# Whole-array transposes and halved products of h in a fused RWKV-7 and SoLU kernel

## The chip, the cores and the metric

The kernel runs on one NeuronCore of a Trainium2 chip. The metric is the device time of one execution in microseconds (us). The core's engines each run a list of instructions of their own: TensorE (PE in the profile; PEld is its loading of weights), VectorE (DVE), ScalarE (ACT), GpSimd (POOL), and SyncE (SP), which here only issues DMAs. TensorE writes its results into PSUM, which ACT and DVE read; a PSUM bank holds 512 fp32 columns.

## The reference

A recurrent attention block feeds an MLP. Everything is fp32 (the two weight matrices arrive as 64-bit floats and are converted on the chip).

```python
B, H, S, D = 4, 8, 768, 40
for t in range(S):                         # state: (B, H, D, D)
    y[:, :, t] = einsum('bhd,bhde->bhe', rt, state)
    Sa = einsum('bhde,bhe->bhd', state, at)
    state = state * wt[:, :, None, :] - einsum('bhd,bhe->bhde', Sa, bt) \
            + einsum('bhd,bhe->bhde', vt, kt)
x = y.transpose(0, 2, 1, 3).reshape(B * S, H * D)      # 3072 x 320
h = x @ w_in                                           # 320 -> 1024
e = exp(h - max(h));  solu = h * e / (sum(e) + 1e-9)
ln = (solu - mean) / sqrt(var + 1e-6) * g_ln
out = ln @ w_out                                       # 1024 -> 320
```

## The kernel before

The 768 time steps are cut into 12 chunks of C = 64, and the four batches into two pairs. One work item is one chunk of one pair: 2 batches x 64 tokens = 128 partitions, batch 0 on partitions 0 to 63 and batch 1 on 64 to 127 (`half(p)`). There are N = 24 items. The recurrence inside a chunk is turned into products of 64x64 matrices and the inverse of a triangular matrix; the inverse is worked out column by column on DVE (`invert`, the groups prod and uu of lines 516 and 519).

All instructions are in a hand-written order, per engine (`manual_schedule`). After a start-up (lines 884 to 970) one loop (line 973) runs i from -1 to 26. Iteration i works on several items at once: it prepares item j = i+5 (decay, transposes of a and b), starts item i+1 (transposes of k, v, r and the state, scores), finishes the attention of item i, and does the MLP of items c = i-2 (h, maximum, exp, variance) and c-1 (transposes and output product). Iterations from i = 5 on (`EARLY - AHEAD`) take the second branch of the loop, which the text calls steady; a steady iteration is the stretch from one transposition of e (tile plnT) to the next.

On TensorE most products are of 64x64 matrices in a quarter of the array, four of them side by side: two halves of the rows (the batch or the head that is contracted) and two halves of the columns. An fp32 product is executed as two passes, so each appears twice in the profile; a transpose appears once.

What the change touches:

- `turned` (line 395) transposes one tensor of 128 tokens x 8 heads x 64 columns. Two heads stand side by side, of which W2 = 104 columns are taken, so there are four blocks; each block is transposed for batch p = 0 and p = 1 by its own instruction. Each loads 64 rows x 104 columns of data as weights and streams the 64 columns of the identity. The two instructions of a block sit on different halves of the array's rows and write to different PSUM banks (`t` is [128, 2, 512]: p chooses the bank, y the 256 columns within). A tensor thus fills half of both banks, and the result is seen as [104, p, j, t].
- It is called by `decay_turned` (tensor ei), `front` (a), `front_b` (b, from the tile kb), `attend_kv` (k from kb, and v), `attend_r` (r) and `stated` (the state, st). Each gives back the copy out of PSUM, which is issued later (on ACT, or on DVE for a and b).
- `folded` (line 794) transposes e, 128 tokens x 1024, in eight blocks of 128 columns for each p into tile plnT; its copy to lnT (line 809) puts the batches side by side. `folded_last` (line 812) does so for the last item, in two tiles.
- `decay_by_halves` (line 368) multiplies the logarithms of the decay with a triangular matrix in 64x64 tiles, the two column halves of 160 in the two banks of the tile that the state's transposes share.
- `hidden` (line 740) does one fifth, n, of h = x @ w_in: four products (row half x, token half y) of 512 columns each. `SPLITS` says how many of the four are done in two of 256 columns instead, for every n and item; its entry 24 holds for all items without an entry of their own.

In a steady iteration TensorE does, in order: transposes of a, b (tile pa), k, v (pkv); the last two of eight output products of an earlier item (po, four records each); transposes of e (plnT), the state (pst), r, ei (pb); the decay products (pst); pu; ps; three fifths of h; and so on to pyo and the first six output products (po).

Of the kernel before, what the change touches and what calls it, by code (L numbers as in the profile page):

```python
# [17 lines left out]
P = 128  # L18
C = 64
# [5 lines left out]
EARLY = 10  # L25
NK = 5
FIRST = 6
SPLITS = {2: (0, 0, 0, 2, 4), 24: (0, 0, 0, 0, 2)}


LN_EXP = "natural_log_exp_and_others"
# [22 lines left out]
def kernel(  # L54
# [18 lines left out]
    nc = tc.nc  # L73
# [6 lines left out]
    NF = DFF // P  # L80
    W2 = C + D
# [17 lines left out]
    def c_(name):  # L99
        lo, hi = where[name]  # L100
        return cst[:, lo:hi]

    ident, tri = c_("ident"), c_("tri")
# [20 lines left out]
    for x in ex_t:  # L124
# [10 lines left out]
                          in_=c_("eye_hi").unsqueeze(1).to_broadcast([P, 8, Q]))  # L135
# [9 lines left out]
    def pair(tag, name):  # L145
        return psum.tile([P, 2, 512], FP32, tag=tag, name=name)
# [121 lines left out]
    def half(p):  # L268
        return slice(C * p, C * p + C)
# [14 lines left out]
    def mm(o, lhsT, rhs, start=True, stop=True):  # L284
        nc.tensor.matmul(o, lhsT=lhsT, rhs=rhs, start=start, stop=stop, skip_group_check=True)  # L285
# [28 lines left out]
    def ok(i):  # L314
        return 0 <= i < N
# [52 lines left out]
    def decay_by_halves(i, t):  # L368

        if not ok(i):  # L370
            return lambda: None
        d = st[i]
        width = DM // 2
        t = t[:, :, 256:256 + width]
        for x in range(2):
            for p in range(2):
                mm(t[half(p), x], c_("cum")[half(p), half(p)], d["lw"][half(p), width * x:width * x + width])

        def evict():
            nc.scalar.activation(out=ei_t[0].rearrange("p (x h) d -> p x h d", x=2)[:, :, :, 0:D],  # L380
                                 in_=t.rearrange("p x (h d) -> p x h d", d=D), func=AF.Exp)
            inv = d["inv"] = two.tile([P, DM], FP32, tag="inv", name="inv", bufs=4)
            nc.scalar.activation(out=inv.rearrange("p (x n) -> p x n", x=2), in_=t, func=AF.Exp, scale=-1.0)
        return evict
# [9 lines left out]

    def turned(t, y, x, skip=0):

        at = 256 * y
        for j in range(4):
            for p in range(2):
                nc.tensor.transpose(out=t[0:W2, p, at + C * j:at + C * j + C],  # L400
                                    in_=x[half(p), 2 * j:2 * j + 2].rearrange("p a b -> p (a b)")[:, skip:skip + W2],
                                    identity=ident[half(p), half(p)])
        return t[0:W2, :, at:at + 256].rearrange("p b (j t) -> p b j t", j=4)

    def tokens(name, bufs=1):
        return two.tile([P, 2, 4, C], FP32, tag=name, name=name, bufs=bufs)
# [6 lines left out]
    def decay_turned(i, t=None, y=0):  # L413

        if not ok(i):
            return lambda: None
        ex = st[i]["ex"] = ex_t[i % (AHEAD + 2)]
        t = turned(pair("B", "pei") if t is None else t, y, ei_t[0])
        return lambda: nc.scalar.copy(out=ex[0:W2, :, :, 1:], in_=t)

    def front(i, t=None, y=0):
        if not ok(i):
            return lambda: None
        d = st[i]
        t = turned(pair("C", "pa") if t is None else t, y, d["raw_a"])
        aT = d["aT"] = tokens("aT", AHEAD)
        return lambda: nc.vector.tensor_tensor(out=aT[0:W2], in0=t, in1=d["ex"][0:W2, :, :, 0:C], op=ALU.mult)

    def front_b(i, t=None, y=0):
        if not ok(i):  # L430
            return lambda: None
        d = st[i]
        t = turned(pair("A", "pb") if t is None else t, y, d["kb"][:, H:])

        def evict():
            if i < EARLY:
                d["bT"] = kept("bT", t)
            else:
                d["bT"] = tokens("bT")
                nc.vector.tensor_copy(out=d["bT"][0:W2], in_=t)  # L440
        return evict
# [132 lines left out]
    def attend_kv(i, t):  # L574

        if not ok(i):
            return lambda: None
        d = st[i]
        for y, x in enumerate((d["kb"], v_t[0])):
            turned(t, y, x)  # L580
        o = two.tile([P, 2, 8, C], FP32, tag="kvT", name="kvT", bufs=1)
        d["kT"], d["vT"] = o[:, :, 0:4], o[:, :, 4:8]
        return lambda: nc.scalar.copy(out=o[0:W2].rearrange("p b j t -> p b (j t)"), in_=t[0:W2])

    def attend_r(i, t, y):
        if not ok(i):
# [153 lines left out]
    def hidden(i, n):  # L740
# [7 lines left out]
        quads = [(y, x) for y in range(2) for x in (y, 1 - y)]  # L748
        whole = len(quads) - SPLITS.get(i, SPLITS[N])[n]
        for part, some in ((slice(0, 512), quads[:whole]), (slice(0, 256), quads[whole:]), (slice(256, 512), quads[whole:])):  # L750
# [43 lines left out]
    def folded(i):  # L794
        if not ok(i):
            return lambda: None
        d = st[i]
        if i == N - 1:
            return folded_last(d)
        lnT = d["lnT"] = two.tile([P, NF, P], FP32, tag="lnT", name="lnT", bufs=1)  # L800
        t = pair("h" if i < N - LAG - 2 else "A" if i == N - LAG - 2 else turn["Y"], "plnT")
        for f in range(NF):
            for p in range(2):
                nc.tensor.transpose(out=t[:, p, f * C:f * C + C], in_=d["e"][half(p), f * P:(f + 1) * P],  # L804
                                    identity=ident[half(p), half(p)])

        def evict():
            o, y = lnT.rearrange("q f (p t) -> q p f t", p=2), t.rearrange("q p (f t) -> q p f t", f=NF)
            nc.scalar.copy(out=o, in_=y)
        return evict  # L810

    def folded_last(d):
        n = NF // 2
        d["lnT"] = (two.tile([P, 2 * n, P], FP32, tag="kvT", name="lnT", bufs=1),
                    two.tile([P, 2 * n, P], FP32, tag="lnT", name="lnT", bufs=1))
        ts = pair(turn["Y"], "plnT"), pair("A", "plnT")
        for f in range(NF):
            for p in range(2):
                nc.tensor.transpose(out=ts[f // n][:, p, f % n * C:f % n * C + C],
                                    in_=d["e"][half(p), f * P:(f + 1) * P], identity=ident[half(p), half(p)])  # L820

        def evict():
            for copy, lnT, t in zip((nc.vector.tensor_copy, nc.scalar.copy), d["lnT"], ts):
                copy(out=lnT[:, 0:n].rearrange("q f (p t) -> q p f t", p=2),
                     in_=t[:, :, 0:n * C].rearrange("q p (f t) -> q p f t", f=n))
        return evict

    def output_last(i):
# [144 lines left out]
    for i in range(-1, N + LAG + 1):  # L973
        j, c = i + AHEAD, i - LAG
# [17 lines left out]
        if i < EARLY - AHEAD:  # L992
            tc_, ta = pair("C", "pa"), pair("A", "pb")
            front_out, r_out = front(j, ta, 0), attend_r(i + 1, ta, 1)
            fold_out = folded(c - 1)
            ei_out, b_out = decay_turned(j + 1, tc_, 0), front_b(j, tc_, 1)
            kv_out = attend_kv(i + 1, pair(turn["X"], "pkv"))
            r_out()
            front_out()
# [11 lines left out]
        else:  # L1011
            turn.update(zip("XY", ("BC", "CB")[(i - EARLY + AHEAD) % 2]))
            ta = pair("A", "pa")
            front_out, b_out = front(j, ta, 0), front_b(j, ta, 1)
            kv_out = attend_kv(i + 1, pair(turn["Y"], "pkv"))
            front_out()
            kv_out()
            b_out()
            if i == N + LAG:
                fold_out = folded(c - 1)  # L1020
# [8 lines left out]
            if i < N + LAG:  # L1029
                fold_out = folded(c - 1)  # L1030
            ts = pair("A", "pst")
# [3 lines left out]
            if i == EARLY - AHEAD and ok(j + 2):  # L1035
                logged(j + 2)
            cum_out = decay_by_halves(j + 2, ts)
            for evict in (r_out, ei_out, fold_out, s_out, *late):
                evict()
# [129 lines left out]
```

## Time and profile before

| | us |
|---|---|
| median of three runs | 538.33 (538.08 to 539.39) |
| span of the profiled execution | 536.5 |
| PE busy | 480.7 |
| DVE busy | 430.6 |
| ACT busy | 314.1 |
| PE, products of h (1064 records) | 121.7 |
| PE, output products po (768 records) | 115.2 |
| PE, transposes of e (368 records, all but the last item) | 16.3 |

The profile is of one execution. Busy time is the union of an engine's instructions, idle time is what lies between them. PE instructions are pipelined: each lasts longer in the records than it keeps the array from the next one, so rates are read from start to start. The times that the three runs show include some time around the span.

### The profile page before, as it was taken

The numbers are of one execution on the slowest core, as the hardware profiler recorded it, in microseconds if no ns is written. First come the engines' busy times: TensorE is split into PE (matmuls) and PEld (weight loads), VectorE is DVE, ScalarE is ACT, GpSimd is POOL, SyncE is SP. The second block draws the span as 40 slices with busy tenths as digits, with TensorE's granted clock in tenths as the row PEclk, the third lists the DMA queues.
The fourth block names the chain that finished last, engine by engine and source line by source line (L and its number), as shares of the span: only waits on it lengthen the run. The fifth ranks groups of instructions, "written<-read, shape, count | busy, mean of one in ns | idle before, by whom it ended". The sixth has DMA issues, their size and how long they took to land.

```text
span 536.5 us, 28053 instructions
## 1 busy us (share of the span) xinstructions
PE 480.7 (90%) x12029; PEld 391.0 (73%) x12029; DVE 430.6 (80%) x1752; ACT 314.1 (59%) x627; POOL 227.0 (42%) x376
## 2 busy tenths in 40 slices
PE   4633775798989999999999999999999999999997
PEld 3522665665878878877887887788778877887766
DVE  4599987999997987997998979979989888544322
ACT  3633466488457566556666665666656555654433
POOL 4577538245253344545445263544445331210300
PEclk9999978799999999999999999999999999999999
DMA  8898889765465566674774776675554551421210
GB/s 149 153 157 160 177 142 206 165 134 124 90 131 120 102 125 138 123 151 96 147 156 104 132 150 121 118 155 109 114 118 102 108 111 43 106 65 29 61 53 24
DMA packets 194475, 63.95 MB, mean 119 GB/s; under 512 B 166840, under 2 KB 186528, under 8 KB 194352
## 3 DMA queue, kind: packets, MB, share of 16 engines
q1 hardware_dynamic: 181232, 41.60, 41.8%
q0 software_dynamic: 10768, 19.95, 15.2%
q8 instruction: 94, 1.54, 1.2%
q10 hardware_dynamic: 2352, 0.62, 0.7%
q14 instruction: 29, 0.24, 0.2%
HBM read 47.96 MB, written 14.16 MB: 116 GB/s over the span
## 4 chain that ended last, share of the span: by engine, by line
PE 73%; DVE 17%; DMA 5%; issue 2%; ACT 2%; SPq 0%; POOL 0%; ACTq 0%; POOLq 0%; DVEq 0%
PE po L285 20%; PE h L285 18%; PE px L285 6%; PE pyo L285 5%; PE py L285 5%; DVE prod L516 4%; PE ps L285 4%; DVE uu L519 3%; PE pu L285 3%; PE plnT L804 2%; PE pb L400 2%; PE pa L400 2%; PE psr L285 2%; PE pkv L400 2%; DMA uu_dram<-uu 1%
## 5 line engine op out<-in xcount | busy, mean ns | idle before, releaser
L285 PE MATMUL h<-w_in,xT 64*64 64x512 f32 (+1 forms) x1064 | 121.7, 551 | 0.7 <-issue 0.7
L285 PE MATMUL po<-w,lnT 128*128 128x160 f32 x768 | 115.2, 304 | 0.0
L516 DVE TENSOR_TENSOR prod<-blk,uu 128x48 f32<-128x48 f32 (+19 forms) x576 | 108.1, 227 | 1.3
L285 PEld LDWEIGHTS po<-w,lnT 128*128 128x128 f32 x768 | 105.5, 190 | 4.7 <-issue 0.8
L519 DVE TENSOR_TENSOR uu<-uu,prod 128x48 f32<-128x48 f32 (+19 forms) x576 | 103.8, 219 | 0.0
L483 POOL DMA_DIRECT2D nt_dram<-nt x86 | 50.8, 597 | 84.5 <-ACT nt L475 76.4
L792 POOL TENSOR_TENSOR rs<-var,mhalf 128x1 f32<-128x1 f32 x24 | 17.6, 734 | 138.2 <-ACT var L791 138.1
L761 DVE TENSOR_REDUCE nmax<-h 128x1 f32<-128x1024 f32 x24 | 29.3, 1219 | 32.9 <-PE h L285 32.9
L285 PEld LDWEIGHTS h<-w_in,xT 64*64 64x64 f32 x1064 | 36.7, 133 | 20.4 <-issue 16.7
L790 ACT ACTIVATE sq<-e,mu 128x1024 f32<-128x1024 f32 x24 | 26.9, 1119 | 24.4 <-DVE e L777 24.4
L444 DVE TENSOR_TENSOR lu<-pu,cst 128x512 f32<-128x512 f32 x24 | 16.5, 686 | 26.6 <-PE pu L285 24.8
L769 ACT ACTIVATE e<-h,nmax 128x1024 f32<-128x1024 f32 x24 | 26.7, 1111 | 17.7 <-DVE nmax L761 17.7
L558 ACT ACTIVATE wy<-py,cst 128x256 f32<-128x256 f32 x24 | 11.4, 474 | 39.2 <-PE py L285 37.1
L311 POOL DMA_DIRECT2D raw_r<-in_r_dram x48 | 33.3, 698 | 0.0
L777 DVE SCALAR_TENSOR_TENSOR e<-h,e 128x1024 f32<-128x1024 f32 x24 | 29.2, 1217 | 4.3 <-ACT e L769 4.1
L508 DVE SCALAR_TENSOR_TENSOR uu<-blk,uu 128x30 f32<-128x30 f32 (+3 forms) x144 | 30.2, 262 | 1.7 <-DMA blk<-nt_dram 0.8
L393 POOL TENSOR_TENSOR kb<-raw_b,inv 128x320 f32<-128x320 f32 x24 | 21.4, 894 | 21.1 <-DMA raw_b<-in_b_dram 13.7
L285 PE MATMUL pcum<-lw,cst 128*128 128x160 f32 x48 | 15.1, 461 | 16.7 <-ACT lw L351 16.7
L285 PEld LDWEIGHTS py<-tu,nt 64*64 64x64 f32 x768 | 17.3, 142 | 16.3 <-issue 10.7
L617 ACT COPY st<-psr 128x416 f32<-128x416 f32 (+1 forms) x44 | 14.2, 374 | 24.5 <-PE psr L285 24.4
L664 ACT ACTIVATE x<-px 128x832 f32<-128x832 f32 x24 | 20.7, 864 | 11.0 <-PE px L285 11.0
L710 DVE TENSOR_TENSOR tot<-pyo,st 104x416 f32<-104x416 f32 x44 | 23.8, 581 | 2.9 <-PE pyo L285 2.9
(154 smaller groups left out, 1095.3 us busy)
## 6 DMA issues: line engine op xcount, KB each, us to landing
xT<-x_dram SPq DMA_DIRECT2D x48, 160.0 KB, 4.2
blk<-nt_dram POOLq DMA_DIRECT2D x22, 256.0 KB, 4.7
raw_w<-in_w_dram SPq DMA_DIRECT2D x48, 80.0 KB, 3.3
raw_r<-in_r_dram POOLq DMA_DIRECT2D x48, 80.0 KB, 4.0
lv<-in_v_dram SPq DMA_DIRECT2D x48, 80.0 KB, 3.7
out_dram<-osb SPq DMA_DIRECT2D x46, 80.0 KB, 2.5
a<-in_a_dram SPq DMA_DIRECT2D x44, 80.0 KB, 4.0
raw_k<-in_k_dram SPq DMA_DIRECT2D x42, 80.0 KB, 3.8
```

The lines of the kernel that those rows point to most:

```text
L285: nc.tensor.matmul(o, lhsT=lhsT, rhs=rhs, start=start, stop=stop, skip_group_check=True)
L311: queue.dma_start(out=x[half(p), :, 0:D], in_=ap[2 * bp + p, :, ci * C:(ci + 1) * C, :].rearrange("h t d -> t h d"))
L400: nc.tensor.transpose(out=t[0:W2, p, at + C * j:at + C * j + C], in_=x[half(p), 2 * j:2 * j + 2].rearrange("p a b -> p (a b)")[:, skip:ski ...
L483: queue.dma_start(out=blocks[n][e].rearrange("(a x h) s c -> a x s h c", a=GRP, x=2)[at, x], in_=nt[home:home + Q].rearrange("p h j c -> p ...
L508: nc.vector.scalar_tensor_tensor(out=u[:, c, j + 1:Q], in0=nb[:, j, j + 1:Q], scalar=u[:, c, j:j + 1], in1=u[:, c, j + 1:Q], op0=ALU.mult, ...
L516: nc.vector.tensor_tensor(out=ts[-1], in0=nb[:, j:j + 1, j + 1:Q].to_broadcast([P, hi - lo, m]), in1=u[:, lo:hi, j:j + 1].to_broadcast([P, ...
L519: nc.vector.tensor_tensor(out=u[:, lo:hi, j + 1:Q], in0=u[:, lo:hi, j + 1:Q], in1=x, op=ALU.add)
L710: nc.vector.tensor_tensor(out=by_b(tot)[:, :, :, part], in0=y[:, :, :, part], in1=by_b(state_of(i)[:, x])[:, :, :, 0:HW], op=ALU.add)
L761: nc.vector.tensor_reduce(out=nmax, in_=d["h"], axis=AX.X, op=ALU.max, negate=True)
L769: nc.scalar.activation(out=e, in_=d["h"], func=AF.Exp, bias=d["nmax"], accum_out=d["esum"])
L777: nc.vector.scalar_tensor_tensor(out=d["e"], in0=d["h"], scalar=1.0 / DFF, in1=d["e"], op0=ALU.mult, op1=ALU.mult, accum_out=d["mu"])
L790: nc.scalar.activation(out=pair("A" if i == N - 2 else "h", "sq").rearrange("p a b -> p (a b)"), in_=d["e"], func=AF.Square, scale=-float( ...
```

## The change

Transposes: one instruction over all 128 partitions takes the place of the two of 64, with a 128-column identity. The four blocks of a tensor lie side by side in one PSUM bank (y chooses the bank), and the two batches are interleaved by block, [104, j, p, t]. The copies read with other strides. `decay_by_halves` moves both its column halves into bank 1 of the tile, as the state now fills bank 0. Products of h: each of the four of each fifth, of every item, is done in two of 256 columns, and the loop of `hidden` itself is unchanged: it runs the four products of the first 256 columns, then the four of the others.

```diff
-SPLITS = {2: (0, 0, 0, 2, 4), 24: (0, 0, 0, 0, 2)}
+SPLITS = {24: (4, 4, 4, 4, 4)}
...
-        t = t[:, :, 256:256 + width]
+        t = t[:, 1].rearrange("p (x n) -> p x n", x=2)[:, :, 0:width]
...
     def turned(t, y, x, skip=0):
 
-        at = 256 * y
         for j in range(4):
-            for p in range(2):
-                nc.tensor.transpose(out=t[0:W2, p, at + C * j:at + C * j + C],
-                                    in_=x[half(p), 2 * j:2 * j + 2].rearrange("p a b -> p (a b)")[:, skip:skip + W2],
-                                    identity=ident[half(p), half(p)])
-        return t[0:W2, :, at:at + 256].rearrange("p b (j t) -> p b j t", j=4)
+            nc.tensor.transpose(out=t[0:W2, y, P * j:P * j + P],
+                                in_=x[:, 2 * j:2 * j + 2].rearrange("p a b -> p (a b)")[:, skip:skip + W2],
+                                identity=ident)
+        return t[0:W2, y].rearrange("p (j b t) -> p b j t", j=4, b=2)
...
-        return lambda: nc.scalar.copy(out=o[0:W2].rearrange("p b j t -> p b (j t)"), in_=t[0:W2])
+        return lambda: nc.scalar.copy(out=o[0:W2], in_=t[0:W2].rearrange("p y n -> p (y n)")
+                                      .rearrange("p (x b t) -> p b x t", x=8, b=2))
...
         t = pair("h" if i < N - LAG - 2 else "A" if i == N - LAG - 2 else turn["Y"], "plnT")
+        t = t.rearrange("q y n -> q (y n)")
         for f in range(NF):
-            for p in range(2):
-                nc.tensor.transpose(out=t[:, p, f * C:f * C + C], in_=d["e"][half(p), f * P:(f + 1) * P],
-                                    identity=ident[half(p), half(p)])
-
-        def evict():
-            o, y = lnT.rearrange("q f (p t) -> q p f t", p=2), t.rearrange("q p (f t) -> q p f t", f=NF)
-            nc.scalar.copy(out=o, in_=y)
-        return evict
+            nc.tensor.transpose(out=t[:, f * P:(f + 1) * P], in_=d["e"][:, f * P:(f + 1) * P], identity=ident)
+        return lambda: nc.scalar.copy(out=lnT.rearrange("q f n -> q (f n)"), in_=t)
...
         for f in range(NF):
-            for p in range(2):
-                nc.tensor.transpose(out=ts[f // n][:, p, f % n * C:f % n * C + C],
-                                    in_=d["e"][half(p), f * P:(f + 1) * P], identity=ident[half(p), half(p)])
+            at = f % n * P
+            nc.tensor.transpose(out=ts[f // n][:, 0, at:at + P], in_=d["e"][:, f * P:(f + 1) * P], identity=ident)
```

The copies of `folded_last` change in the same way.

More of the change, by code (lines that the diff above doesn't have):

```diff
@@ L817, in folded_last @@
         for f in range(NF):
-            for p in range(2):
-                nc.tensor.transpose(out=ts[f // n][:, p, f % n * C:f % n * C + C],
-                                    in_=d["e"][half(p), f * P:(f + 1) * P], identity=ident[half(p), half(p)])
+            at = f % n * P
+            nc.tensor.transpose(out=ts[f // n][:, 0, at:at + P], in_=d["e"][:, f * P:(f + 1) * P], identity=ident)
         def evict():
             for copy, lnT, t in zip((nc.vector.tensor_copy, nc.scalar.copy), d["lnT"], ts):
-                copy(out=lnT[:, 0:n].rearrange("q f (p t) -> q p f t", p=2),
-                     in_=t[:, :, 0:n * C].rearrange("q p (f t) -> q p f t", f=n))
+                copy(out=lnT[:, 0:n].rearrange("q f t -> q (f t)"), in_=t[:, 0])
         return evict
```

## The prediction

> **What bounds the kernel now.** I read the summary page first (busy shares, the slices, the chain that ended last), then the busy time by stretches, then TensorE in order of time inside one steady iteration. The page:
>
> ```profile
> PE 480.7 (90%) x12029; PEld 391.0 (73%) x12029; DVE 430.6 (80%) x1752; ACT 314.1 (59%) x627; POOL 227.0 (42%) x376
> ...
> PE   4633775798989999999999999999999999999997
> ...
> PE 73%; DVE 17%; DMA 5%; issue 2%; ACT 2%; SPq 0%; POOL 0%; ACTq 0%; POOLq 0%; DVEq 0%
> ```
>
> From the ninth of 40 slices on PE stays at 8 tenths or more, and 73% of the chain is PE. The stretches tell where that holds (columns: stretch, its length, busy PE, PEld, DVE, ACT, POOL, clock, DMA):
>
> ```profile
> 107.00:126.00 19.00, 16.12 (x432) 10.96 (x432) 18.83 (x79) 16.68 (x35) 7.95 (x13) 1.00 0.67 142
> 126.00:147.00 21.00, 20.59 (x506) 16.31 (x508) 20.79 (x64) 12.21 (x26) 8.34 (x12) 1.00 0.49 99
> 281.50:300.00 18.50, 18.50 (x512) 15.37 (x514) 15.27 (x66) 11.95 (x24) 9.42 (x15) 1.00 0.57 114
> ```
>
> Up to 147 us DVE is the full one (20.79 of 21.00) and the chain runs through it from about 100 us; after that PE is busy 18.50 of 18.50 and DVE has 3 us to spare per iteration. So from 147 us (iteration i=4) to the end, what the change does to PE's own stream is what it does to the time. A stretch of that stream (start, length to the last end, instruction, count; each ordinary fp32 matmul is recorded twice, a transpose once):
>
> ```profile
> 294.08 3.53 PE L285 MATMUL po<-w,lnT 128*128 128x160 f32 x24
> 297.54 0.43 PE L400 MATMUL pa<-cst,a 64*104 64x64 f32 x8
> 297.81 0.39 PE L400 MATMUL pa<-cst,kb 64*104 64x64 f32 x8
> 298.03 0.39 PE L400 MATMUL pkv<-cst,kb 64*104 64x64 f32 x8
> 298.26 0.39 PE L400 MATMUL pkv<-cst,v 64*104 64x64 f32 x8
> 298.57 1.35 PE L285 MATMUL po<-w,lnT 128*128 128x160 f32 x8
> 299.86 0.71 PE L804 MATMUL plnT<-cst,e 64*128 64x64 f32 x16
> 300.41 0.39 PE L400 MATMUL pst<-cst,st 64*104 64x64 f32 x8
> 300.63 0.40 PE L400 MATMUL pb<-cst,r 64*104 64x64 f32 x8
> ```
>
> A record lasts longer than it holds the array; what counts is from start to next start. Eight transposes, four pairs on the two halves of the rows, advance the stream by 0.22 us (298.03 to 298.26, 300.41 to 300.63): 0.0555 us a pair. The plnT pairs (0.55 us for eight, 0.05 of it the first load) take 0.062. A po record of 160 columns takes (1.35 - 0.40) / 7 = 0.136, its first lasting 0.40.
>
> **Transposes over the whole array.** This is the large term. Where two instructions of 64 moving columns ran side by side, one of 128 columns runs alone. What sets a pair's 0.0555: the columns that stream, or the weights that load (104 columns)? By the po row 160 columns cost 0.136, 0.83 ns a column and 0.002 between records. Priced so, 64 columns take 0.053 + 0.002 = 0.055, just what a pair takes. Three more rows speak for streaming. In the trace's own starts near 123.9 us the two halves run out of step (123.903, 123.936, 123.959, 123.992): each keeps its 0.056 rhythm though the other starts 0.023 after it, so each half is held by its own 64 columns, and they do not take turns. And where TensorE runs at half pace early on (the granted clock shows nothing of it, the spacing does):
>
> ```profile
> 13.79 0.67 PE L400 MATMUL pa<-cst,a 64*104 64x64 f32 x8
> 14.25 0.63 PE L400 MATMUL pb<-cst,kb 64*104 64x64 f32 x8
> ```
>
> starts there are 0.1067 apart (14.036, 14.143, 14.249, 14.356): 64 columns at twice 0.833 ns, nothing over. And after an empty array the second load starts 0.045 after the first where 104 columns are loaded (300.596, 300.641) and 0.060 with plnT's 128 (299.856, 299.916): the load of 104 is done before the rhythm of 0.0555 needs it; only plnT's 0.062 is the load's. So I price a whole transpose as 128 streamed columns, 128 x 0.833 + 0.002 = 0.109 us. The other bound is 0.0555 (0.062 for plnT), if loads set it; the four rows put it near the upper one.
>
> Per full steady iteration there are 28 pairs (a, b, k, v, state, r, ei at four each) and 8 of plnT: 28 x 0.0532 + 8 x 0.047 = 1.49 + 0.37 = +1.86 us.
>
> **Borders between tilings.** Now each switch of the array's layout empties it. The last po before 297.54 starts at 297.31 (its end less 0.30), an unbroken stream would go on at 297.45, and the first pair's load is bare for 0.05 more: 0.15 us. From pkv to po: 298.26 + 0.22 = 298.48, but po starts at 298.57 and its first record is 0.10 long with a bare load: 0.20. po to plnT: 0.15 again. After the change po and the transposes all use the whole array, so these three go: -0.50 us per iteration. The border from ei to the 64-row decay products stays. No row shows a transpose next to a product in one layout, so the gain lies between 0 and 0.50; pyo (64 rows, 104 columns) to po leaves the same 0.09 with no transpose in it, so I take the layout as the cause and 0.50. The Trainium skill, "TensorEngine Tiling (Array Packing)", Key Properties, says that changing the tiling mode drains TensorE; the trace agrees, with 0.09 us, and by the rule the sum keeps the 0.50.
>
> **Products of h in 256 columns.** An undivided product (8 records of 512) advances 0.86. Now the last of five is half divided, and the last product of chunk 2 is divided whole:
>
> ```profile
> 158.16 1.11 PE L285 MATMUL h<-w_in,xT 64*64 64x256 f32 x14
> 159.00 0.50 PE L285 MATMUL py<-uh,wy 64*64 64x32 f32 x20
> ...
> 309.65 1.07 PE L285 MATMUL h<-w_in,xT 64*64 64x512 f32 x12
> 310.54 0.65 PE L285 MATMUL py<-uh,wy 64*64 64x32 f32 x30
> ```
>
> Half divided takes 309.65 to 310.54 = 0.89. Wholly divided, its sets of four come 0.2155 apart, 4 x 0.2155 = 0.862 (158.11, the first, to 159.00 is 0.89 with 0.03 of a bare first load). So four products gain 0.006 each and the fifth gives back 0.026: 0 per iteration. Between -0.03 x 24 = -0.7 and, if each pays the bare load, +0.03 x 120 = +3.6 us in all; I take 0, as products in the steady stream have their weights loaded ahead. In records the change is even: 1712 transposes become 856, and 1064 h records become 1920.
>
> **At nothing.** The copies move as many elements in other strides: the strided lnT copy takes 1.03 us and the contiguous kvT copy of as many 1.01, so a pattern is worth 0.02; they run on ACT (11.95 of 18.50) and DVE (15.27) beside PE, and would cost if they came late: the copy of lnT ends at 303.28 and h's first product, in the same banks, starts at 303.41, and the three copies before that start keep their distance to ei's last transpose; each 0.1 us that lnT's copy came late would cost 0.1 in 17 iterations, 1.7. The decay halves go to one bank; both row halves already write one bank side by side, and the two column halves of one row half already follow one another: 0 (if they came to take turns, 8 records of 0.135 in 12 iterations, +6.5 at most).
>
> **Sum**, against the profiled span of 536.5: i=5, which has no leftover po, 1.86 - 0.15 = 1.7; i=6 to 17, 12 x 1.36 = 16.3; i=18 without ei 1.15; i=19 to 22 (16 pairs and plnT) 4 x (0.85 + 0.37 - 0.50) = 2.9; i=23 to 26, plnT alone, 1.0. Together 23.1. Before 147 us DVE covers most. The chain has 24 pairs there, in five places up to 67 us, at half pace, 24 x 0.107 = 2.6 at most; i=4 adds up to 1.7; the four iterations between, 4 x 1.36 = 5.4 if DVE gave no cover. I take half of the first two and none of the third: 2.2. In all +25.3, span 561.8. The run's median is 538.33, 1.8 above the span, so **563.5 us**.
>
> **Rivals.**
> First, faster: the pair's rhythm is set by its weight load, so a whole transpose takes no longer than a pair (0.0555 to 0.062). Then only the borders count: 17 iterations x 0.50, and 0.6 at i=5 and in the tail, -9, giving 531. It decides if a whole transpose advances the stream by under about 0.07 us (36 x 0.014 = 0.50). For it: plnT's rhythm is its load's, so the two are near each other. Against it: the half-pace rows and the halves out of step. 0.12. The Trainium skill, "TensorE: Matmul & The Clock Gate", Terms, calls transpose mode four times faster for fp32, which against two records of 0.83 ns a column would be 0.42 ns, and so this rival; the trace's 64 columns in 0.055 show twice, not four times.
>
> Second, slower still: going from product to transpose empties the array whatever the layout, and the 0.50 stays. 17 x 0.50 + 0.6 = 9 more: 572.5. Nothing in the trace shows such a border, for or against. 0.18.
>
> Third, the change costs nothing that can be seen, since the longer transposes fall into waits of PE. PE's idle stretches after 170 us sum to about 1.2 us, so hardly: 538, 0.02.
>
> **How the numbers follow.** Forecast 0.68. It lies between 558 (early part free, PE's idle taken up, 2 us from copies and order that I can't price) and 571 (early part whole); the second rival reaches 575 and lies within its spread, so 554 to 575 holds about 0.8. This kernel's runs differ by 0.3%, 1.6 us. Slower 0.86, the same 0.02, faster 0.12.
>
> **What would show it.** After, transposes 128*104 128x128: eight (kb and v) should advance by 0.87 us, not 0.44; plnT's eight by 0.87. No idle of PEld between po and pa, pkv and po, po and plnT. A steady iteration of 18.46 us (plnT to plnT) should become 19.8. An h product stays at 0.86. If transposes advance by 0.055 to 0.065, the first term is wrong and the time falls; if idle of 0.09 stays at the borders, the second.

## The result, and the profile after

The changed kernel takes 563.52 us (median of six runs, 561.18 to 566.24) against 538.38 beside it: 1.0474 of the time before, 95% interval 1.0447 to 1.0500. 563.5 was forecast. Single runs of some kernels below fell into a slower state of the chip (the longest took 805 us at a granted clock of 0.58); ratios, medians and ranges here leave them out. The profiled execution has a span of 560.9 us, 24.4 more than before. From the summary page of the changed kernel:

```profile
PE 511.9 (91%) x12029; PEld 459.9 (82%) x12029; DVE 430.4 (77%) x1752; ACT 315.2 (56%) x627; POOL 222.5 (40%) x376
...
PE   4553776989999999999999999999999999999997
...
PE 79%; DVE 8%; DMA 6%; SPq 3%; ACT 2%; issue 1%; ACTq 0%; DVEq 0%
```

As many instructions on every engine as before; DVE and ACT work about as long as before, and PE's share of the chain has grown from 73% to 79%. The same place of a steady iteration, TensorE in order of time (start, length, instruction, count):

```profile
303.88 3.53 PE L285 MATMUL po<-w,lnT 128*128 128x160 f32 x24
307.24 0.60 PE L398 MATMUL pa<-cst,a 128*104 128x128 f32 x4
307.68 0.60 PE L398 MATMUL pa<-cst,kb 128*104 128x128 f32 x4
308.12 0.60 PE L398 MATMUL pkv<-cst,kb 128*104 128x128 f32 x4
308.55 0.60 PE L398 MATMUL pkv<-cst,v 128*104 128x128 f32 x4
308.99 1.25 PE L285 MATMUL po<-w,lnT 128*128 128x160 f32 x8
310.08 1.04 PE L803 MATMUL plnT<-cst,e 128*128 128x128 f32 x8
310.95 0.60 PE L398 MATMUL pst<-cst,st 128*104 128x128 f32 x4
311.39 0.60 PE L398 MATMUL pb<-cst,r 128*104 128x128 f32 x4
```

Four transposes advance the stream by 0.44 us (307.24, 307.68, 308.12, 308.55, 308.99), 0.109 each, where four pairs took 0.22; eight of plnT take 0.87, where they took 0.55. Blocks of 104 and of 128 loaded columns now have one rhythm, so it is the streamed columns that set it and not the load. And the borders are gone: po starts at 308.99, where v's fourth transpose ends its 0.109, and its eight records take 1.25, not 1.35. The iteration from 290.13 to 310.08 us (columns as in the stretches shown of before):

```profile
290.13:310.08 19.95, 19.95 (x511) 18.45 (x509) 15.31 (x65) 11.94 (x25) 9.26 (x16) 1.00 0.55 111
```

PE is still never idle and DVE still works 15.3 us, now of 19.95.

### The profile page after: what moved, and what is told of

It reads as the page before. It is cut to its first block, busy times and chain, and to the rows that moved or that the text cites. A ratio compares the mean times of both kernels' runs of the same rounds, so it can differ in the third digit from the quotient of the medians.

```text
span 560.9 us, 28063 instructions
## 1 busy us (share of the span) xinstructions
PE 511.9 (91%) x12029; PEld 459.9 (82%) x12029; DVE 430.4 (77%) x1752; ACT 315.2 (56%) x627; POOL 222.5 (40%) x376
## 3 DMA queue, kind: packets, MB, share of 16 engines
q0 software_dynamic: 10768, 19.95, 14.4%
## 4 chain that ended last, share of the span: by engine, by line
PE 79%; DVE 8%; DMA 6%; SPq 3%; ACT 2%; issue 1%; ACTq 0%; DVEq 0%
PE po L285 19%; PE h L285 18%; PE pyo L285 6%; PE px L285 6%; PE py L285 5%; PE plnT L803 4%; PE ps L285 3%; PE pkv L398 3%; PE pb L398 3%; PE pu L285 3%; PE pa L398 3%; DMA uu_dram<-uu 2%; DVE prod L514 2%; DVE uu L517 2%; PE psr L285 2%; PE pst L398 2%
## 5 line engine op out<-in xcount | busy, mean ns | idle before, releaser
L285 PE MATMUL h<-w_in,xT 64*64 64x256 f32 x1920 | 123.1, 378 | 0.1
L285 PE MATMUL po<-w,lnT 128*128 128x160 f32 x768 | 113.4, 302 | 0.0
L517 DVE TENSOR_TENSOR uu<-uu,prod 128x48 f32<-128x48 f32 (+19 forms) x576 | 109.9, 231 | 0.0
L514 DVE TENSOR_TENSOR prod<-blk,uu 128x48 f32<-128x48 f32 (+19 forms) x576 | 103.7, 221 | 1.3
L285 PEld LDWEIGHTS h<-w_in,xT 64*64 64x64 f32 x1920 | 68.5, 133 | 18.6 <-issue 0.8
L791 POOL TENSOR_TENSOR rs<-var,mhalf 128x1 f32<-128x1 f32 x24 | 13.6, 566 | 136.9 <-ACT var L790 136.9
L581 ACT COPY kvT<-pkv 104x1024 f32<-104x1024 f32 x24 | 24.4, 1016 | 13.5 <-PE pkv L398 13.5
L408 ACT COPY rT<-pb 104x512 f32<-104x512 f32 x24 | 14.1, 586 | 29.3 <-PE pb L398 29.3
L393 POOL TENSOR_TENSOR kb<-raw_b,inv 128x320 f32<-128x320 f32 x24 | 21.3, 887 | 21.8 <-DMA raw_b<-in_b_dram 13.7
L285 PE MATMUL pcum<-lw,cst 128*128 128x160 f32 x48 | 13.9, 432 | 14.3 <-ACT lw L351 14.3
```

The costliest lines, as they stand in the source:

```text
L514: nc.vector.tensor_tensor(out=ts[-1], in0=nb[:, j:j + 1, j + 1:Q].to_broadcast([P, hi - lo, m]), in1=u[:, lo:hi, j:j + 1].to_broadcast([P, ...
L517: nc.vector.tensor_tensor(out=u[:, lo:hi, j + 1:Q], in0=u[:, lo:hi, j + 1:Q], in1=x, op=ALU.add)
L581: return lambda: nc.scalar.copy(out=o[0:W2], in_=t[0:W2].rearrange("p y n -> p (y n)") .rearrange("p (x b t) -> p b x t", x=8, b=2))
```

## The experiments

Ratios are to runs of the kernel before on the same chip, whose median went from 536.2 to 539.3 us between chips. A "clean" iteration is the shortest full steady one, plnT to plnT: 18.46 us before, 19.86 in the changed kernel (+1.40), each reached within 0.01 in five iterations. Others are longer, some with no idle time in the profile, as the end of a matmul is modelled and hides a short wait.

**Only the transposes.** The changed kernel with the old division of h:

```diff
-SPLITS = {24: (4, 4, 4, 4, 4)}
+SPLITS = {2: (0, 0, 0, 2, 4), 24: (0, 0, 0, 0, 2)}
```

> The changed kernel with the products of h divided as they were before the change. Theory: the transposes carry the slowdown, and dividing h costs 0.027 us per item (five fifths of h take 4.354 us in the changed trace, 4.327 before), so this takes 563.5 - 24 x 0.027 = 562.9 us, 24.5 above the kernel before. Rival: the halved products carry a share, by records issued or weights loaded twice as often; then this falls well below, at 560 or less.

Measured: 561.15 us, 1.0418 (1.0396 to 1.0441); clean iterations +1.38. So the transposes carry the slowdown. By the total, 21.8 us above the kernel before on its chip, it lies 2.7 under the theory (24.5) and beside the rival (21.6 or less). The iterations speak for the theory: clean ones differ from the changed kernel's by 0.02. Where the rest lies is not settled, as the profile is of the longest of its five runs; single iterations in it have idle time of a kind to which the next runs lead.

**Only the halved products of h.** The same line the other way round, in the kernel before:

> The kernel before with every product of h in two of 256 columns. Theory: +24 x 0.027 = +0.65 us, 539.0. The prediction's own term was 0 (538.4), with +3.6 (542.0) as its upper end.

Measured: 558.62 us (554.50 to 561.57), 1.0355 (1.0316 to 1.0394). A clear miss of theory and prediction: halving h alone costs 19 us, three quarters of what the whole change costs. The same kernel was run a second time, for another profile:

> The kernel before with every product of h halved, a second time, for another profile. Theory of the blocks: an iteration has 1096 entries, not 1024, so the borders wander through it; idle time of TensorE with no wait in the profile stands at the entry 64 before each border (place 193 of 256) and nowhere else, and iterations without it are 0.02 to 0.03 us longer than before; 554 to 562 us. Rival, that the halved products themselves are slow: every iteration is longer by the same 0.8 us.

Measured: 551.92 us, 1.0294 (1.0225 to 1.0363). Of its steady iterations the clean ones are 0.02 us longer than before, others up to 2.2 us. TensorE in order of time in one of these; the bracket gives the idle time before the group and what ended it:

```profile
200.86 0.50 PE L285 MATMUL py<-tu,nt 64*64 64x32 f32 x23
202.47 0.36 PE L285 MATMUL py<-tu,nt 64*64 64x32 f32 x9 [1.11 <-issue]
202.62 1.11 PE L285 MATMUL h<-w_in,xT 64*64 64x256 f32 x16
```

In the middle of 32 equal small products, with their operands long there, PE stands still for 1.11 us, and "issue" means that no semaphore explains it. Count the entries of TensorE's list in the trace: a product is a load and a matmul, each of them twice, and a wait for a semaphore that has an instruction of its own is one more. Then all 19 waits of 0.1 us or more that no semaphore explains between 110 and 450 us, 11.5 us together, stand before an entry whose number leaves 193 when divided by 256. The other idle time there ends with work of ACT or DVE, as the state's 0.5 us at i=5, and stands at other numbers. The same holds of the kernel before (four waits, 2.9 us) and of every kernel below. The DMA queue that fetches TensorE's instructions moves 16 KB a packet, 94 packets in the kernel before for some 24,200 entries, 101 here for 25,900: 256 to a packet. At the end of each of the 19 waits exactly as many packets had started as 256 goes into the entry's number, the last of them 2.3 to 3.0 us ahead of that end. So TensorE waits for its own instructions. A steady iteration of the kernel before has 508 matmul records, as many loads and 8 waits of their own: 1024 entries, exactly four blocks, whose borders (taken at the places 193) fall at the same four places each time (ps, px, py, and the transposes of v); the shortest block takes 3.7 us. The change keeps the count (1024 or 1025 by turns), as 36 transposes fewer make room for 36 records of h more. Halving h alone makes it 1096, and the borders wander, also into places where 256 entries are worked off in 3.0 us.

**The transposes in two parts.** First the seven tensors of `turned` with e left in pairs, then e alone. The first kernel also has every product of h halved, which its expectation does not say; the second divides h as before:

```diff
-SPLITS = {2: (0, 0, 0, 2, 4), 24: (0, 0, 0, 0, 2)}
+SPLITS = {24: (4, 4, 4, 4, 4)}
...
+            nc.tensor.transpose(out=t[0:W2, y, P * j:P * j + P],
+                                in_=x[:, 2 * j:2 * j + 2].rearrange("p a b -> p (a b)")[:, skip:skip + W2],
+                                identity=ident)
...
+            nc.tensor.transpose(out=t[:, f * P:(f + 1) * P], in_=d["e"][:, f * P:(f + 1) * P], identity=ident)
```

> The kernel before with the seven tensors of 104 columns transposed over the whole array, and e still in pairs. Theory (whole transposes stream 0.0532 us more than a pair, and each border between layouts costs 0.15 to 0.20): per steady iteration 28 x 0.0532 = 1.49, less the borders po to pa (0.15) and pkv to po (0.20), plus a new one from plnT to pst (0.15): +1.29. Times 12, plus 1.1 at i=18, 4 x 0.65 after it, and 1.7 for everything up to i=5: +20.9, 559.3 us. Rival, that borders do not follow the layout but come with any turn from products to transposes: +1.49 each, +24, 562.

Measured: 572.30 us, 1.0620 (1.0584 to 1.0655). The cleanest full iteration is 1.31 longer than before. The theory has 1.29 for the transposes, and the halved products add 0.02 to a clean iteration (by the second of the two runs above), 1.31 in all; the rival would be at 1.51. The total is 13.7 above the kernel with only h halved, run on the same chip. It can't be set against the 559.3, which leaves the halved products out: an iteration has 1040 or 1041 entries, and 14 waits of 0.1 us or more at the place 193 between 110 and 450 us come to 8.6 us of idle time.

> The kernel before with only e transposed over the whole array. Theory: 8 x 0.047 = +0.37 us per iteration; the border po to plnT goes (-0.15) and one from plnT to pst comes (+0.15). 17 iterations x 0.37 + 1.2 at the ends = +7.5, 545.9 us; together with the kernel that transposes only the other seven this is 28.4 over the kernel before, 4 to 5 more than both do in one, as the borders around plnT are paid in each. Rival without borders: the two add up to the whole, 24.

Measured: 549.28 us, 1.0192 (1.0164 to 1.0220). Clean iterations +0.36 (expected 0.37); the total is 3 us over, again with block waits (1008 entries). Clean, the two parts make 1.31 + 0.36 = 1.67, the halved products counted once, where the changed kernel, with both and the halved products, makes 1.40: the 0.27 more are the two borders around plnT, po to plnT and plnT to the state, one of which each half-changed kernel has (0.30 expected).

**The borders without the transposes.** All eight output products at the end of the iteration, so that no po stands between the transposes; first in the kernel before, then in the changed one:

```diff
-FIRST = 6
+FIRST = 8
```

> The kernel before with all eight output products at the end of the iteration, none left over between the transposes of v and of e. Theory: the borders pkv to po (0.20) and po to plnT (0.15) go, -0.35 in 17 iterations, -6.0 us, but the state's transposes, whose tile waits for DVE's copy of b, then stand 0.5 us before that copy ends (it would end near 300.62 where they could start at 300.07), so about +0.2 is left per iteration: 538 to 542. Rival, no such wait: 532.4. Rival, borders cost nothing: 538.4 with no wait, 547 with it.

Measured: 540.17 us, 1.0069 (1.0043 to 1.0095), within what the theory gave. Its reason is in the order of time:

```profile
278.25 0.67 PE L804 MATMUL plnT<-cst,e 64*128 64x64 f32 x16
279.45 0.43 PE L400 MATMUL pst<-cst,st 64*104 64x64 f32 x8 [0.53 <-DVE bT L440]
```

plnT now follows v by 0.22 (v starts at 278.03), with no border: that saves the 0.35. But the state's transposes start 1.20 after plnT, where in the next kernel but one the transposes behind plnT start 0.49 after it: 0.71 is lost to DVE's copy of b, 0.53 of it as idle time. Clean iterations come out at +0.39, where the theory had left 0.2.

> The changed kernel with no output products left over. Here po and the transposes use the array in one layout, so there is no border to remove, and the longer transposes give DVE's copies time: 563.5, within 1. If what goes in the kernel before were not the border but the order itself, this would fall by the same 6 us.

Measured: 562.80 us, 1.0486 (1.0450 to 1.0521): no gain, as expected where there is no border to remove.

With the state's transposes moved behind those of r and ei as well, in the kernel before:

```diff
+            tc_ = pair(turn["X"], "pb")
+            r_out, ei_out = attend_r(i + 1, tc_, 0), decay_turned(j + 1, tc_, 1)
             ts = pair("A", "pst")
             s_out = stated(i + 1, ts, 0) if ok(i + 1) else lambda: None
-            tc_ = pair(turn["X"], "pb")
-            r_out, ei_out = attend_r(i + 1, tc_, 0), decay_turned(j + 1, tc_, 1)
```

> As the kernel with no output products left over, and the transposes of the state after those of r and ei instead of before them, so that DVE's copy of b has 0.44 us more. Theory: borders -0.35, a wait of 0.1 left: -0.25 in 17 iterations, 534 us. If borders cost nothing: 538 to 540.

Measured: 534.48 us, 0.9954 (0.9934 to 0.9973), faster than both kernels. A full iteration of it:

```profile
278.02 0.66 PE L804 MATMUL plnT<-cst,e 64*128 64x64 f32 x16
278.51 0.39 PE L400 MATMUL pb<-cst,r 64*104 64x64 f32 x8
278.74 0.39 PE L400 MATMUL pb<-cst,ei 64*104 64x64 f32 x8
279.21 0.43 PE L400 MATMUL pst<-cst,st 64*104 64x64 f32 x8
```

The number fits, its working only in part: in full iterations the state still starts 0.25 late for b's copy, and most of them come out level with before (18.40 to 18.65). The gain stands in the last iterations with attention (0.6 us at i=17, and 0.6 in the three from i=19 on, which have no a or b to wait for), at i=5 (0.7, where the kernel before waits for b's copy), and in three iterations (1.1, 1.2 and 0.8) in which the kernel before waits for instruction blocks (in the second for ACT and DVE as well) and this one less or not at all. That the sum came out at 534 is luck.

**No product of h divided.** `SPLITS = {24: (0, 0, 0, 0, 0)}` in the kernel before:

> The kernel before with no product of h divided. The last fifth of h takes 0.888 half divided and 0.894 wholly divided; the 0.03 above 0.86 is the first load, bare behind products of 32 columns. Theory: undivided it takes 0.887, no change, 538.4. Rival, that it is the division that costs: 0.857, -0.03 x 24 = -0.7, 537.7.

Measured: 543.28 us, 1.0119 (1.0098 to 1.0141). Clean iterations are level with before to 0.01, so for h itself the theory holds. The total is 6 us over: 1016 entries in an iteration, and waits of 0.1 to 1.1 us at the place 193.

**The block borders moved, the work kept.** One item's products of h divided otherwise, in the kernel before and in the changed one:

```diff
-SPLITS = {2: (0, 0, 0, 2, 4), 24: (0, 0, 0, 0, 2)}
+SPLITS = {2: (4, 4, 4, 4, 4), 24: (0, 0, 0, 0, 2)}
...
-SPLITS = {24: (4, 4, 4, 4, 4)}
+SPLITS = {2: (0, 0, 0, 0, 0), 24: (4, 4, 4, 4, 4)}
```

> The kernel before with the products of h of one item alone, item 2, all divided: 14 more matmuls, 56 more entries in TensorE's stream, once. The other items and the 1024 entries of a steady iteration stay. Theory, that TensorE's instructions come in blocks of 256 and a block worked off in less than about 3.7 us is waited for: the block borders move by 56 entries, and the shortest block of each steady iteration falls from 3.7 to 3.0 us in the trace of before (13 blocks of 3.02, 13 of 3.64 between 170 and 430 us): 13 x 0.7 + 13 x 0.06 = +10 us, 547, with TensorE idle at the entry before each border of 256 less 63. Rival, that the idle time in the kernel with all products halved comes from its own products (banks, loads): +0.03 us, no change.

Measured: 542.68 us, 1.0079 (1.0054 to 1.0104). 14 matmuls in one item cost 4 us, most of it (3.4) spread over iterations 6 to 13, after that item's products in iteration 4: the rival falls. Little of it shows as idle time, but matched matmul by matmul with a clean iteration, these fall behind mostly just after the places 193. The size is less than half of what was expected, and the working had the shift the wrong way round (56 entries more put the borders 56 earlier in the old list, where 14 blocks take 3.07 and no others less than 3.7).

> The changed kernel with the products of h of item 2 alone undivided: 20 matmuls, 80 entries of TensorE's stream fewer, once. Theory of the blocks: 13 blocks of a steady stretch shrink from 3.5 to 2.95 us, +7 to +9 us, 571. Rival: no change, 563.5.

Measured: 571.02 us, 1.0613 (1.0570 to 1.0656), 7.5 more than the changed kernel (ratios compared, as the chips differ) for 20 matmuls fewer. The number fits, though with the shift read aright it is other blocks that shrink (by the trace of the changed kernel, 38 of the 39 between 170 and 430 us to under 3.8 us). What one short block costs is therefore not settled: several blocks of 3.07 to 3.5 us went by without a visible wait, so the blocks before a short one seem to count too. That was not tried.

## Why the prediction was right

| part | predicted | measured |
|---|---|---|
| start to plnT of i=5 | 2.2 | 1.07 |
| i=5 | 1.7 | 0.72 |
| i=6 to 17 | 16.3 | 16.99 |
| i=18 to 22 | 4.1 | 4.70 |
| i=23 to the end | 1.0 | 0.95 |
| sum | 25.3 | 24.43 |

(measured: how much later each transposition of e starts, from plnT to plnT, and the end)

The mechanism was right: TensorE sets the time from i=6 on, a whole transpose costs its 128 streamed columns, and the borders go. That the total met the forecast to 0.1 us is luck, as misses cancel: the first two rows are 2.1 too dear, the rest 1.2 too cheap (waits for instruction blocks at i=19 and 21 alone make 1.0), and the runs' median stands 2.6 above the profiled span where 1.8 was added. (The sum as written also gives 563.6, and the first rival's 9 us less than 538.3 would be 529, not 531.)

*The transposes' price* was right to the nanosecond: 0.109 us, for 104 and for 128 loaded columns. The rows that decided it, the equal price per column of po, the two halves out of step, the second load after 0.045, spoke of streaming, and the first rival falls. The fourfold speed of fp32 transposes in the Trainium skill (TensorE: Matmul & The Clock Gate, Terms) is not seen here: 0.85 ns a column, against 1.67 for an fp32 product's two passes, is twofold.

*The borders*: all three are gone, with no idle time where a transpose meets a product in one layout, so the second rival (572.5) falls as well. Their price was tested: 0.27 measured for two of them in the half-changed kernels, 0.30 predicted. For all three, the 1.86 of the longer transposes less the 1.38 of the kernel with only the transposes changed leaves 0.48; 0.50 was predicted.

*The products of h* were put at 0 per iteration and cost 0.027: the five fifths take 4.354 us after and 4.327 before. The term gave back 0.026 in the last fifth; it did not come, since the bare first load (0.03) stands there whether the product is divided or not, behind products of 32 columns. That is 0.65 us in all. What the prediction put at nothing without a word is the waits for instruction blocks, which cost the halved products alone 16 to 19 us. It had remarked that the records come out even, but tied no cost to it. Nor is it evenness that decides: the kernel with only the transposes changed has 952 entries in an iteration, not four blocks, and no more waits. Over clean time, iterations 6 to 17 take about 2.5 us more in the kernel before, 2.7 in the changed one and 2.5 in that one, so the term is near nothing in the difference. That is luck too: with its list shifted by 80 entries the changed kernel takes 571 us.

*The terms at nothing* held: the lnT copy takes 1.03 us in both kernels and h starts 0.13 after it, and the decay products in one bank take 0.47 as before.

*The early part* was too dear. It was priced at half pace, +0.107 for each transpose (the chain's rows up to 67 us hold 28 pairs, not 24, so 3.0 at most). At plnT of i=3, 126 us, the changed kernel is only 0.03 us behind. Part of the reason is in the last section: between 13.4 and 20.2 us it runs at full pace, and what it lost before is made up by 16.2 us. But the 0.03 itself is not a measure: the last kernel of the experiments, whose list is the same up to there, comes to this point 1.0 us earlier.

*i=5* costs 0.72, not 1.7: in the kernel before this iteration is 0.68 over a clean one, since the state's transposes wait for DVE's copy of b (0.53 us idle), so PE was not the bound there, and that much of the 1.40 fell into the wait.

*i=18* was priced with 24 pairs beside those of e, but without a and b it has 16, and costs 0.75, not 1.15.

*The third rival*, that waits swallow the cost, holds in part up to i=5, and nowhere else.

## What to carry to other kernels

Price a transpose by its streamed columns, from a row of an ordinary product on the same chip, and check by the load which of the two sets the rhythm. Here columns set it, and 28 pairs of transposes on half the rows side by side beat 28 on the whole array although each change of layout costs 0.15 to 0.20 us. Where TensorE is never idle, find where the blocks of 256 entries of its list end, before and after a change: a few instructions more, anywhere ahead, move every later border. Over all thirteen profiles, between 150 and 440 us, a visible wait of 0.1 us or more follows 35 of the 67 blocks worked off in under 3.2 us, 45 of 256 between 3.2 and 3.8, and 3 of 281 over 4.5. So the 3.7 us of the expectations is no sharp limit.

## What was not expected of the hardware

**Instruction blocks.** The waits above reach 1.4 us (in the second profile of the halved products) and make kernels whose clean iterations differ by 0.02 us differ by 3% and more in all. They may also widen the spread of the runs, which was not shown: 0.3% before (up to 0.8 on other chips), 0.9% in the changed kernel, 1.3% with the halved products alone. The Trainium skill (Runtime: NRT & Kernel Launch, Instruction fetch mechanics) describes the 16 KB blocks of 256 instructions and calls the cost of crossing a border mostly hidden; the size agrees with the packets here, the hiding does not.

**The pace of TensorE early on.** The same products at the start, first in the kernel before, then in the changed one:

```profile
14.25 0.63 PE L400 MATMUL pb<-cst,kb 64*104 64x64 f32 x8
14.81 1.43 PE L285 MATMUL pcum<-lw,cst 128*128 128x160 f32 x4
16.18 1.13 PE L285 MATMUL py<-aT,bT 40*64 40x64 f32 x32
```

```profile
14.84 0.60 PE L398 MATMUL pb<-cst,kb 128*104 128x128 f32 x4
15.27 0.71 PE L285 MATMUL pcum<-lw,cst 128*128 128x160 f32 x4
16.16 0.69 PE L285 MATMUL py<-aT,bT 40*64 40x64 f32 x32 [0.18 <-ACT bT L408]
```

In the kernel before TensorE runs at half pace here: pcum takes 1.43 us, against 0.71 in the changed kernel, whose four whole transposes of 0.109 take no longer than the four pairs of 0.107. The changed kernel comes to full pace by 13.5 us, after three tensors' transposes end to end at half pace (8.73 to 11.3 us, 0.21 to 0.22 each). It does not last: at 25 us the 32 products py take 1.14 us in both kernels. The granted clock (third column from the right) seems to read the other way, first the kernel before, then the changed one:

```profile
22.00:66.90 44.90, 21.51 (x383) 18.19 (x385) 42.60 (x204) 17.92 (x39) 27.57 (x40) 1.00 0.92 166
66.90:73.70 6.80, 4.42 (x203) 3.90 (x200) 4.65 (x20) 5.90 (x12) 0.00 (x0) 1.00 0.88 162
73.70:80.50 6.80, 5.91 (x113) 5.12 (x112) 6.70 (x31) 3.53 (x7) 4.10 (x8) 0.50 0.74 125
```

```profile
8.00:13.40 5.40, 4.87 (x49) 4.31 (x48) 0.69 (x1) 3.02 (x8) 0.86 (x1) 1.00 0.81 172
13.40:20.20 6.80, 4.58 (x71) 3.48 (x64) 3.07 (x6) 5.71 (x12) 5.85 (x9) 1.00 0.96 161
20.20:44.10 23.90, 14.47 (x114) 11.78 (x112) 21.70 (x94) 10.19 (x21) 15.27 (x24) 0.50 1.02 170
```

The trace's records of the clock settle it. The first one begins at 66.9 us in the kernel before and at 13.4 in the changed one, each with full pace; ahead of it there is none, and the profile puts 1.00 there though the products run at half pace. From the first record on the two agree: 0.50 goes with half pace, 1.00 with full. So the lower means of the runs (0.947 against 0.984) do not say that the changed kernel is slower early on; its half pace is merely on record from 20.2 us, that of the kernel before from 73.7. All records but the last of a run last a multiple of 3.41 us. In the four other kernels with whole transposes of the seven tensors the first begins at 10 to 13 us, in the seven others without at 64 to 68. That longer activity is what brings the pace was not tested by itself.
